# Softmax without the row-maximum pass in a two-block attention kernel, with a check of the row sums and a general program beside it

## The chip, the cores and the metric

The kernel runs on one core of one Trainium2 chip. The time is device microseconds (us) of one execution; medians of several executions are quoted, and one more execution of each kernel was recorded with a profile and a trace. All profiled executions and all timed ones named here were at a mean granted TensorE clock of 0.96 to 1.00. Engine names are those of the profile: PE is TensorE and PEld its weight loads, DVE is VectorE, ACT is ScalarE, POOL is GpSimd, SP is SyncE, SPq the queue of loads that SyncE issues.

## The reference

Two attention blocks over cached keys and values, A with grouped heads and B with one key and value head for each query head, their outputs set side by side:

```python
# A: Hq=32, Hkv=4 (each key/value head serves 8 query heads); B: 32 heads of each
# both: B=16, Sq=32, D=1024, Sk=1024, Dh=128, everything in bfloat16
q = (x @ wq).reshape(B, Sq, Hq, Dh).transpose(0, 2, 1, 3)
k = jnp.repeat(k_cache, rep, axis=1)          # rep = 8 in A, no repeat in B
v = jnp.repeat(v_cache, rep, axis=1)
scores = jnp.einsum("bhqd,bhkd->bhqk", q, k) * (Dh ** -0.5)
p = jax.nn.softmax(scores, axis=-1)
o = jnp.einsum("bhqk,bhkd->bhqd", p, v)
out = o.transpose(0, 2, 1, 3).reshape(B, Sq, Hq * Dh) @ wo
# ... and jnp.concatenate([a, b], axis=-1)
```

Inputs are normal numbers times 0.1, so the scores are small. B's keys and values are 268 MB of the 338 MB that have to be read.

## The kernel before

The work is cut into 128 "quads" of A and 128 of B. A quad is a block of 128 rows by 1024 scores: scores (TensorE), maximum (VectorE), exponential with row sum (ScalarE), transposes of P (TensorE), P times V (TensorE), normalisation, a transpose of the result, and now and then a projection. B's keys are transposed by VectorE, A's by TensorE. One load of 1 MB brings B's keys of a quad into one of two slots.

```python
NVB_SLOTS = 3
NKB_SLOTS = 2
DMA_BW = 330.7e3                      # bytes per us that the scheduler assumes
DUR = {                               # durations that the scheduler assumes, us
    "scoresB": 1.1, "scoresA": 0.45, "PT_trA": 0.50, ...
    "exp": 1.12, ...
    "KBt_tr": 1.15, "max": 1.17, "recip": 0.07, ...
}
# ... cut ...
def st_ktrB(q, t_):                   # frees the key slot rs
    sl, rs = q.kvslot, q.krslot
    pr.add("dve", lambda e: e.transpose(KBt_sb[:, sl, t_, :].bitcast(F32), KB_sb[:, rs, t_, :].bitcast(F32)),
           reads=[("KB", rs)], writes=[("KBt", sl, t_)], name="KBt_tr", ...)
# ... cut ...
def st_max(q):                        # minus scale times the row maximum, into stat
    sbf, sl = q.sbuf, q.slot
    pr.add("dve", lambda e: e.tensor_scalar(P_sb[:, sl, :], ps_s[:, sbf, :, :].rearrange("p u n -> p (u n)"), -scale, None,
                                            ALU.mult, ALU.min, accum_out=stat[:, sl, 0:1]),
           writes=BK_S[sbf] + [("nbias", sl), ("P", sl)], name="max", ...)

def st_exp(q):
    ...
    pr.add("act", lambda e: e.activation(dst, src, ACTF.Exp, bias=stat[:, sl, 0:1], scale=scale, accum_out=stat[:, sl, 1:2]),
           reads=[("nbias", sl)], writes=BK_S[sbf] + [("P", sl), ("rowsum", sl)], name="exp", ...)
```

Nothing of this is emitted as it is written. `pr.add` records operations with what they read and write. A list scheduler then goes through them with a small model: one in-order queue for each engine, the durations of `DUR`, one DMA pipe of `DMA_BW`. At each step it takes the ready operation with the earliest start (within 0.35 us, the one with the longest path behind it). The order it finds is emitted, with semaphore waits where the records ask for them.

```python
def list_schedule(self, lat=0.12, dma_bw=DMA_BW, dma_lat=1.8, look=0.35):
    # ... cut ...
    seq = sorted(range(n), key=lambda k: (ops[order[k]].t0, k))
    newp = Prog()
    for k in seq:
        eng, emit, reads, writes, dma_key, name, dur, tag, prio = self.specs[order[k]]
        newp.add(eng, emit, reads, writes, dma_key, name, dur, tag, prio)
    return newp
```

So an operation that is taken out of the program is also taken out of the scheduler's model, and every engine's order may come out differently.

## Time and profile before

| | before |
|---|---|
| median of the runs | 997.39 us at first, 995.62 with the later run (988.38 to 999.15) |
| span of the profiled run | 994.8 us |
| DMA queue of loads | 92.8% of 16 engines' span, 339.78 MB |
| VectorE, TensorE, ScalarE busy | 782.3, 863.6, 605.3 us |
| idle DMA, from stretches of 2 us | 11.3 us before 76 us, 59.4 in the middle, 19.3 in the last 75 |

The last line is read this way: cut the span into stretches of 2 us, take the DMA share of each, and add up what it lacks to 1. The prediction shows the other lines and how they hang together. These are the main rows of before's waits that belong to the softmax (columns: the waiter, whom it waited for, us in total, times, longest):

```profile
ACT P_sb L792 <- DVE P_sb L780: 99.6, 107, 5.6
...
PEld ps_pt L806 <- ACT P_sb L792: 26.4, 39, 3.1
...
DVE stat L843 <- ACT P_sb L792: 16.8, 26, 1.5
```

The first row is the exponential behind the maximum. The second is the transpose of P on TensorE, which needs the exponential's result; the third the reciprocal on VectorE, which needs its row sum.

### The profile page before, as it was taken

What the parts mean: (1) busy time and instruction counts of PE and PEld (TensorE: products, weight loads), DVE (VectorE), ACT (ScalarE), POOL (GpSimd) and SP (SyncE); (2) the same over time, 40 slices, a digit from 0 to 9 for tenths busy, and PEclk for the clock granted to TensorE, in tenths of its full rate; (3) what the DMA queues carried; (4) which work ended last, traced back from release to release, by engine and by line L of the source; (5) the groups of instructions that cost most, each with busy time, mean ns of one, the idle gap of its engine ahead of it and who ended that gap; (6) DMA issues with size and microseconds to landing.
All of it is one profiled execution on the core that took longest, in us unless ns stands there. A gap on an engine that the chain in (4) does not pass through costs nothing.

```text
span 994.8 us, 29548 instructions
## 1 busy us (share of the span) xinstructions
PE 863.6 (87%) x12864; PEld 480.5 (48%) x12864; DVE 782.3 (79%) x1460; ACT 605.3 (61%) x1237; POOL 1.1 (0%) x8
## 2 busy tenths in 40 slices
PE   5789999998998899998898989899988888888766
PEld 3345554555554555555454445455554445454332
DVE  2468787788887889888888788788887878988763
ACT  2247676766675667666575567657565656676332
POOL 0000000000000000000000000000000000000000
PEclk7999999999999999999999999999999999999875
DMA  8889899989999889999899997999999889999993
GB/s 306 306 300 375 327 352 349 386 329 357 355 350 393 331 323 389 357 366 366 315 382 384 344 354 268 347 378 349 357 368 386 306 316 363 377 352 354 337 339 141
DMA packets 151936, 341.66 MB, mean 343 GB/s; under 512 B 10496, under 2 KB 26880, under 8 KB 151808
## 3 DMA queue, kind: packets, MB, share of 16 engines
q1 hardware_dynamic: 151808, 339.78, 92.8%
q8 instruction: 101, 1.65, 0.7%
q14 instruction: 27, 0.22, 0.1%
HBM read 337.64 MB, written 2.10 MB: 342 GB/s over the span
## 4 chain that ended last, share of the span: by engine, by line
PE 47%; DVE 33%; ACT 14%; issue 2%; DMA 2%; SPq 0%; DVEq 0%; ACTq 0%
DVE P_sb L780 14%; DVE KBt_sb L733 12%; PE ps_s L769 9%; PE ps_pt L806 9%; ACT P_sb L792 8%; PE ps_pj L624 6%; PE ps_o L824 5%; PE ps_pj L546 4%; PE ps_pj L563 4%; ACT PT_sb L477 3%; PE ps_o L834 3%; PE ps_s L747 3%; DVE acc L637 2%; PE ps_o L860 2%; ACT KTA_sb L477 1%
## 5 line engine op out<-in xcount | busy, mean ns | idle before, releaser
L780 DVE TENSOR_SCALAR_CACHE_REDUCE P_sb<-ps_s 128x1024 bf16<-128x1024 f32 x256 | 310.0, 1213 | 80.5 <-PE ps_s L747 31.7
L792 ACT ACTIVATE P_sb<-ps_s,stat 128x1024 bf16<-128x1024 f32 x256 | 285.5, 1116 | 115.1 <-DVE P_sb L780 99.6
L733 DVE STREAM_TRANSPOSE KBt_sb<-KB_sb 128x1024 f32<-128x1024 f32 x256 | 309.8, 1226 | 5.9 <-PE ps_s L769 5.2
L477 ACT COPY PT_sb<-ps_pt 128x512 f32<-128x512 f32 x256 | 149.8, 585 | 92.6 <-PE ps_pt L806 74.2
L806 PE MATMUL ps_pt<-id,P_sb 128*128 128x128 f32 x1024 | 185.9, 305 | 19.7 <-ACT P_sb L792 13.7
L806 PEld LDWEIGHTS ps_pt<-id,P_sb 128*128 128x128 f32 x1024 | 149.8, 209 | 58.4 <-ACT P_sb L792 26.4
L769 PE MATMUL ps_s<-KBt_sb,QR 32*32 32x512 bf16 x4096 | 159.4, 402 | 18.0 <-DVE KBt_sb L733 12.8
L834 PE MATMUL ps_o<-VB_sb,PT_sb 128*32 128x128 bf16 x4096 | 85.8, 225 | 12.8 <-DVE OTA_sb L479 5.9
L747 PE MATMUL ps_s<-KTA_sb,QT_sb 128*128 128x512 bf16 x256 | 86.8, 385 | 5.1 <-ACT KTA_sb L477 1.6
L849 ACT ACTIVATE O_sb<-ps_o,stat 128x128 bf16<-128x128 f32 x128 | 47.2, 369 | 71.3 <-PE ps_o L824 64.4
L834 PEld LDWEIGHTS ps_o<-VB_sb,PT_sb 128*32 128x32 bf16 x4096 | 62.0, 99 | 56.8 <-issue 47.6
L769 PEld LDWEIGHTS ps_s<-KBt_sb,QR 32*32 32x32 bf16 x4096 | 49.6, 90 | 77.1 <-issue 25.5
L824 PE MATMUL ps_o<-VA_sb,PT_sb 128*128 128x128 bf16 x1024 | 79.7, 221 | 7.1 <-ACT OTB_sb L477 5.1
L824 PEld LDWEIGHTS ps_o<-VA_sb,PT_sb 128*128 128x128 bf16 x1024 | 62.9, 99 | 42.4 <-ACT OTB_sb L477 21.2
L624 PE MATMUL ps_pj<-woB_sb,OTB_sb 128*128 128x512 bf16 x256 | 76.7, 403 | 5.5 <-DVE ost L640 1.9
L563 PE MATMUL ps_pj<-wq_sb,xT_sb 128*128 128x512 bf16 x256 | 72.1, 392 | 5.5 <-ACT QR L477 3.5
L624 PE MATMUL ps_pj<-woA_sb,OTA_sb 128*128 128x512 bf16 x256 | 70.1, 382 | 6.4 <-DVE OTA_sb L479 5.7
L860 PE MATMUL ps_o<-ident,O_sb 128*128 128x128 bf16 x256 | 58.3, 228 | 18.0 <-DVE O_sb L853 15.4
L546 PE MATMUL ps_pj<-xT_sb,wq_sb 128*128 128x512 bf16 x256 | 68.8, 387 | 4.8 <-ACT QR L477 1.7
L860 PEld LDWEIGHTS ps_o<-ident,O_sb 128*128 128x128 bf16 x256 | 25.1, 98 | 81.5 <-DVE O_sb L853 38.6
L477 ACT CAST QR<-ps_pj 128x256 bf16<-128x256 f32 x128 | 48.0, 375 | 23.7 <-PE ps_pj L583 22.5
L853 DVE TENSOR_SCALAR O_sb<-ps_o,stat 128x128 bf16<-128x128 f32 x128 | 42.7, 334 | 17.8 <-PE ps_o L834 17.2
(37 smaller groups left out, 599.9 us busy)
## 6 DMA issues: line engine op xcount, KB each, us to landing
KB_sb<-in_B_k_cache_dram SPq DMA_DIRECT2D x128, 1024.0 KB, 7.3
VB_sb<-in_B_v_cache_dram SPq DMA_DIRECT2D x256, 512.0 KB, 8.5
KA_sb<-in_A_k_cache_dram SPq DMA_DIRECT2D x64, 256.0 KB, 9.0
VA_sb<-in_A_v_cache_dram SPq DMA_DIRECT2D x64, 256.0 KB, 8.5
wq_sb<-in_B_wq_dram SPq DMA_DIRECT2D x32, 256.0 KB, 8.2
wq_sb<-in_A_wq_dram SPq DMA_DIRECT2D x32, 256.0 KB, 7.5
woB_sb<-in_B_wo_dram SPq DMA_DIRECT2D x32, 256.0 KB, 9.6
woA_sb<-in_A_wo_dram SPq DMA_DIRECT2D x32, 256.0 KB, 8.6
```

Source lines behind the costliest of these rows:

```text
L477: pr.add("act", lambda e: e.copy(dst_ap, src_ap), reads=reads, writes=writes, name=name + "@act", wtag=wtag, rtag=rtag)
L546: last = e.matmul(ps_pj[:, 0:tn], wq_sb[:, 0, j, hc * Dh:(hc + 1) * Dh], xT_sb[:, 0, j, t0:t0 + tn], start=(j == 0), stop=(j == DJ - 1))
L563: last = e.matmul(ps_pj[:, 0:CW], xT_sb[:, 1, j, G * P:(G + 1) * P], wq_sb[:, 1, j, :], start=(j == 0), stop=(j == DJ - 1))
L624: last = e.matmul(ps_pj[:, 0:OUTW], OT[:, gp, hh, :], wo_[:, hh, oh * OUTW:(oh + 1) * OUTW], start=(hh == 0), stop=(hh == nh - 1))
L733: pr.add("dve", lambda e: e.transpose(KBt_sb[:, sl, t_, :].bitcast(F32), KB_sb[:, rs, t_, :].bitcast(F32)), reads=[("KB", rs)], writes=[(" ...
L747: pr.add("pe", lambda e, u=u: e.matmul(ps_s[:, sbf, u, :], qt[:, q.b, q.hh0:q.hh0 + 4, :].rearrange("p a q -> p (a q)"), KTA_sb[:, sl, u * ...
L769: last = e.matmul(ps_s[32 * cg:32 * cg + 32, sbf, g2, :].rearrange("p (s j) -> p s j", s=16), lhsT, rhs, start=(fp == 0), stop=(fp == 3), ...
L780: pr.add("dve", lambda e: e.tensor_scalar(P_sb[:, sl, :], ps_s[:, sbf, :, :].rearrange("p u n -> p (u n)"), -scale, None, ALU.mult, ALU.mi ...
L792: pr.add("act", lambda e: e.activation(dst, src, ACTF.Exp, bias=stat[:, sl, 0:1], scale=scale, accum_out=stat[:, sl, 1:2]), reads=[("nbias ...
L806: last = e.transpose(ps_pt32[:, m * P:(m + 1) * P], p32[:, m:Sk // 2:NPK], id32[:])
L824: last = e.matmul(OREG[0][0][:, 0:Dh], ptc, VA_sb[:, kvs, c, :], start=(c == 0), stop=(c == NCH - 1))
L834: last = e.matmul(ps_o[32 * a:32 * a + 32, 0:Dh], ptc, VB_sb[:, kvs, a // 2, a % 2, c, :], start=(c == 0), stop=(c == NCH - 1), tile_posit ...
```

## The change

The intent: softmax gives the same result with any constant subtracted in place of the maximum as long as nothing overflows or vanishes. The changed kernel subtracts nothing, so VectorE loses 256 passes over 128x1024 scores, and the exponential loses its wait for them. To stay right for any input, the reciprocals of all row sums are kept and compared with two limits at the end; if one lies outside, a slow general program with the maximum runs in the same launch.

```diff
+RINV_LOW, RINV_HIGH = 1e-10, 1e10
@@ ... cut ...
+    def whole(name, eng):
+        fast.run_engine(name, eng, fast_sems)
+        eng.wait_ge(fast_sems[flag_op.eng], flag_op.sig)
+        reg = eng.alloc_register("flag_" + name)
+        eng.reg_load(reg, flag[0:1, 0:1])
+        if name == "sp":
+            fast.await_dmas(eng, fast_sems)
+        with eng.If_ne(reg, flag_good):
+            eng.drain().then_inc(meet, 1)
+            eng.wait_ge(meet, len(engines))
+            general.run_engine(name, eng, general_sems)
@@ ... cut: the general program ...
-        def st_max(q):
-            sbf, sl = q.sbuf, q.slot
-            pr.add("dve", lambda e: e.tensor_scalar(P_sb[:, sl, :], ps_s[...], -scale, None, ALU.mult, ALU.min, accum_out=stat[:, sl, 0:1]), ...)
@@ st_exp
-            pr.add("act", lambda e: e.activation(dst, src, ACTF.Exp, bias=stat[:, sl, 0:1], scale=scale, accum_out=stat[:, sl, 1:2]),
-                   reads=[("nbias", sl)], writes=BK_S[sbf] + [("P", sl), ("rowsum", sl)], name="exp",
+            pr.add("act", lambda e: e.activation(dst, src, ACTF.Exp, scale=scale, accum_out=stat[:, sl, 1:2]),
+                   writes=BK_S[sbf] + [("P", sl), ("rowsum", sl)], name="exp",
@@ st_recip
-            pr.add("dve", lambda e: e.reciprocal(stat[:, sl, 2:3], stat[:, sl, 1:2]), ...)
+            pr.add("dve", lambda e: e.reciprocal(q.rinv, stat[:, sl, 1:2]), ...)      # a column of rinv_all
@@ before the scheduler
+        def st_check():
+            # ... cut: two comparisons of rinv_all with accum_out into good[:, 0:1] and good[:, 1:2], a memset of ones ...
+            pr.add("pe", lambda e: e.matmul(ps_pj[0:1, 0:2], ones[:], good[:], start=True, stop=True), ...)
+            # ... cut: two products on VectorE ...
+            pr.add("dve", lambda e: e.tensor_copy(flag[:], good[0:1, 1:2]), reads=[("good", 1)], writes=["flag"], name="flag")
+        st_check()
+        pr = pr.list_schedule()
```

`DUR` and `DMA_BW` stay as they were. The scheduler runs on a program in which the maximum does not exist.

## The prediction

> **What bounds the kernel now.** I read the page first, then the DMA queue's own waits, then stretches of 25 us and of 2 us, then the timeline where the DMA falls idle. From the page, engine totals, the load queue and the chain of waits:
>
> ```profile
> PE 863.6 (87%) x12864; PEld 480.5 (48%) x12864; DVE 782.3 (79%) x1460; ACT 605.3 (61%) x1237; POOL 1.1 (0%) x8
> ...
> q1 hardware_dynamic: 151808, 339.78, 92.8%
> ...
> PE 47%; DVE 33%; ACT 14%; issue 2%; DMA 2%; SPq 0%; DVEq 0%; ACTq 0%
> DVE P_sb L780 14%; DVE KBt_sb L733 12%; PE ps_s L769 9%; PE ps_pt L806 9%; ACT P_sb L792 8%; PE ps_pj L624 6%; PE ps_o L824 5%; PE ps_pj L546 4%; PE ps_pj L563 4%; ACT PT_sb L477 3%; PE ps_o L834 3%; PE ps_s L747 3%; DVE acc L637 2%; PE ps_o L860 2%; ACT KTA_sb L477 1%
> ...
> L780 DVE TENSOR_SCALAR_CACHE_REDUCE P_sb<-ps_s 128x1024 bf16<-128x1024 f32 x256 | 310.0, 1213 | 80.5 <-PE ps_s L747 31.7
> L792 ACT ACTIVATE P_sb<-ps_s,stat 128x1024 bf16<-128x1024 f32 x256 | 285.5, 1116 | 115.1 <-DVE P_sb L780 99.6
> L733 DVE STREAM_TRANSPOSE KBt_sb<-KB_sb 128x1024 f32<-128x1024 f32 x256 | 309.8, 1226 | 5.9 <-PE ps_s L769 5.2
> ```
>
> No engine fills the span, but the DMA engines nearly do: 92.8% for loads alone. The chain blames TensorE and VectorE in turns; its 14% on the maximum (L780) is 139 us, which is an upper bound and not the gain, since a DMA at 92.8% stands beside it. The maximum and the transpose of B's keys (L733) are two equal blocks on one in-order VectorE.
>
> The link between VectorE and the DMA is in the DMA queue's own waits (columns: waiter and releaser, us in total, times, longest):
>
> ```profile
> SPq L700 <- DVE KBt_sb L733: 262.3, 67, 13.6
> SPq L700 <- DVE stat L843: 112.7, 22, 10.1
> SPq L700 <- DVE O_sb L853: 54.1, 14, 7.7
> ```
>
> L700 loads a megabyte of B's keys into one of two slots; a slot is free once VectorE has transposed it. The names behind the arrow are whichever VectorE instruction brought its counter to the awaited value. That wait is harmless while the queue still has transfers to work off. Two stretches of 25 us show when it is not (the last columns are granted clock, DMA share, GB/s):
>
> ```profile
> 300.00:325.00 25.00, 21.47 (x314) 12.34 (x314) 19.17 (x36) 14.70 (x32) 0.00 (x0) 1.00 1.04 392
> 600.00:625.00 25.00, 22.89 (x354) 12.78 (x353) 21.23 (x39) 16.14 (x33) 0.00 (x0) 1.00 0.75 271
> ```
>
> At 300 the DMA runs full at 392 GB/s; at 600 it is empty for a quarter of the time, and TensorE is no less busy. I cut the first 960 us into stretches of 2 us: in 358 of 480 the share was at least 0.98, at a mean of about 387 GB/s; the shortfall of the others from a share of 1 adds up to 75 us: 11 before 76 us, 59 between 76 and 920, 5 after. I looked at what the queue waited for in 14 places where the share fell: in 13 it was an L700 load released by VectorE. One of them, around 570 us:
>
> ```profile
> 567.90 1.23 DVE L780 TENSOR_SCALAR_CACHE_REDUCE P_sb<-ps_s 128x1024 bf16<-128x1024 f32 x1 [0.71 <-PE ps_s L769]
> ...
> 569.78 2.36 DVE L733 STREAM_TRANSPOSE KBt_sb<-KB_sb 128x1024 f32<-128x1024 f32 x2
> ...
> 572.17 0.37 SPq L700 DMA_DIRECT2D KB_sb<-in_B_k_cache_dram  x1
> ```
>
> The DMA share is 0.09 at 570 to 572. The two transposes stand behind the maximum and its wait for scores; the load goes out the moment they end.
>
> **What the Trainium skill says.** "VectorE: DVE Perf Modes", section on the TRN2 errata, gives 120 + elements cycles at 0.96 GHz for a source in PSUM: 1192 ns for 1024 elements at one per cycle. The trace has 1213, so the maximum is already at the rate of its form and only its removal helps. "ScalarE: Activation LUTs", section "What ACT_TABLE_LOAD costs", puts about 93 ns on each per-partition pointer operand of an activation. The trace agrees: the 128x128 normalisation with a pointer scale takes 369 ns, the 128x128 copy 269. "DMA: Bandwidth & Descriptors", Specifications, names about 358 GB/s as a core's HBM limit; this trace holds 392 over 25 us with one core running, so I use the measurement. "Runtime: NRT & Kernel Launch", "Instruction fetch mechanics", says a taken branch outside the prefetched window must fetch its target before execution goes on, without a figure; no such branch is in this trace.
>
> **The change part by part.**
>
> 1. Removed: 256 maxima of 1213 ns and 256 accumulator reads of 83 ns on VectorE: 310 + 21 = 331 us. VectorE falls to 782 - 331 = 451 us, under half of any likely span.
>
> 2. Removed from each softmax: 1.2 us plus 0.1 between the scores and the exponential, and VectorE's queueing on top. ScalarE's idle time before exponentials caused by the maximum, 99.6 us, should vanish; part of it returns as a wait for scores.
>
> 3. The built program gives the exponential an immediate bias in place of a pointer. At about 95 ns each, 256 of them take 24 us off ScalarE: 1116 to about 1020 ns, ScalarE 605 to about 581 us. It was idle 39% of the time, so this alone is worth little.
>
> 4. Added: results of the reciprocal go to columns of one tile (same size, no cost); two checks of 128x256, one 1x2 matmul, three tiny VectorE operations, and one register load, compare and taken branch on every engine. In the instruction order, the matmul and the last three VectorE operations stand behind the last accumulation, beside the last store, which took some 2.7 us in the trace (992.1 to 994.8). I estimate 1 to 4 us for what sticks out, 2.5 in the middle. The general program is skipped; its instructions cost only the jump.
>
> 5. Moved: the scheduler rebuilds the order. The counts on TensorE and the DMA queue stay the same apart from the check, and A's work stays in the same ratio to B's (17 quads of A by B's 16th, 122 by its 112th), so I expect no new shape.
>
> What then sets the end? TensorE: from start-to-start distances around 500 to 510 us, B's 32 score matmuls take 1.07 us, B's values 0.57, four transposes of P about 0.6, A's scores 0.43, A's values 0.45, a transpose of A's keys 0.45 per two quads, the shuffle 0.22, the output transposes 0.06 each, and eight projection matmuls 1.72: about 6.0 us per pair, times 128 is 770 us of dense work. The DMA needs 341.66 MB / 387 GB/s = 883 us. So the DMA is the next bound, TensorE comes 13% behind it.
>
> The sum: 883, plus 2 before the first byte, plus some 19 after the last load has landed (about 976 to 994.8), is 904 us, a floor. The span of 994.8 lies 91 above it: 75 of idle DMA, and 16 of reduced rate. Idle DMA in the middle, 59, should shrink to about 20, since VectorE's other in-order waits for TensorE and ScalarE stay in front of the transposes (saves 39). The start, paced by TensorE's projections and small loads, gives back 2; reduced rate 5; the B-only end 1.5; the last two softmaxes in the drain 2.4. Together 50, less 2.5 for the check: 47.5. From the median of 997.4: about 950 us.
>
> **The rivals.**
>
> The DMA is hidden-bound already and VectorE's load is worth nothing. For it: 92.8%, and the megabytes stay. Against it: 13 of 14 gaps end with VectorE, and full stretches run 14% faster than the mean of 343 GB/s. It would leave 985 to 995 us.
>
> The wait moves to TensorE: key slots still free late, because transposes stand behind reciprocals, normalisations and accumulations that wait for matmuls, and value slots (L713, L707) wait for TensorE as now (39.7 and 25.0 us). For it: TensorE is 87% busy and its share is rarely under 80%. Against: 770 us of dense work. It would keep most of the 59 and give 965 to 980.
>
> The full gain: two in-order engines stop blocking one another and the DMA saturates through the middle: 905 to 925 us. For it: stretches such as 300 to 325 do that with VectorE at 77%.
>
> A dear exit, with tens of us for branch and fetch, would be seen only at the end; I give it little.
>
> **Range and chances.** Between the full gain and TensorE's in-order waits I take 950, and 925 to 975 eight times in ten; the three times before themselves differ by 1%. Two per cent faster means under 977.4: only the first rival, or the second at its worst, fails that. Faster 0.91, same 0.08, slower 0.01.
>
> **What would show it.** Right: DMA share of loads 96 to 98% and a mean near 360 GB/s; VectorE near 450 us; exponential near 1020 ns; the L700 wait on VectorE well under 262 us; the chain of waits with no maximum and more TensorE, and DMA above its 2%. Wrong: a rate in full stretches under 380 GB/s (contention), the share still 93% with gaps released by TensorE (second rival), or an exit of over 5 us after the last store.

## The result, and the profile after

The changed kernel's median is 958.87 us (955.75 to 961.89, 4 runs), before's in the same session 995.62. Ratios here are the mean time of one kernel's fast runs over that of the other's of the same rounds, so they are not quite the ratio of the medians; for the change it is 0.964 (95% interval 0.9588 to 0.9692). The result is correct, and the general program did not run.

The page of the changed kernel, engine totals, the load queue, the chain of waits and two groups:

```profile
PE 850.0 (89%) x12866; PEld 473.5 (49%) x12866; DVE 503.5 (53%) x955; ACT 576.0 (60%) x1237; POOL 1.3 (0%) x10
...
q1 hardware_dynamic: 151808, 339.78, 94.9%
...
PE 65%; ACT 24%; DVE 6%; issue 2%; DMA 2%; SPq 0%; POOLq 0%; DVEq 0%
...
L846 DVE STREAM_TRANSPOSE KBt_sb<-KB_sb 128x1024 f32<-128x1024 f32 x256 | 308.3, 1225 | 38.3 <-PE ps_s L882 27.2
L899 ACT ACTIVATE P_sb<-ps_s 128x1024 bf16<-128x1024 f32 x256 | 263.8, 1030 | 83.3 <-PE ps_s L882 53.7
```

VectorE is free for half of the span, and its share of the chain fell from 33% to 6%. The exponential (L899) takes 1030 ns in place of 1116. But the loads fill only 94.9%, and the chain went to TensorE and ScalarE, not to the DMA, whose 2% did not move. The question for the trace is who empties the DMA now. Two stretches of 25 us, the same as in the prediction (the last columns are granted clock, DMA share, GB/s):

```profile
300.00:325.00 25.00, 23.19 (x329) 12.71 (x327) 12.97 (x26) 14.37 (x31) 0.00 (x0) 1.00 1.05 410
600.00:625.00 25.00, 22.53 (x347) 12.93 (x344) 13.44 (x27) 17.32 (x37) 0.00 (x0) 1.00 0.93 342
```

The same parts of the work do not lie at quite the same times, so this shows only the kind: a full stretch runs at 410 GB/s, and others are still not full. By stretches of 2 us the idle DMA of the middle fell from 59.4 to 42.8 us, that of the last 75 us from 19.3 to 12.9, that of the start stayed (11.3 and 11.6). The load queue's own waits in the changed kernel:

```profile
SPq L813 <- DVE KBt_sb L846: 189.4, 54, 13.7
SPq L813 <- DVE rinv_all L950: 188.6, 41, 8.9
SPq L813 <- DVE OTA_sb L590: 56.2, 16, 7.6
SPq L826 <- PE ps_o L941: 49.3, 30, 5.6
```

L813 is the load of B's keys. The names behind the arrow can't be taken at their word. In the built program every such load that waits for VectorE waits for the count of a key transpose; and in the trace 121 of the 126 loads that reuse a slot start within 0.1 us of the end of that slot's second transpose (116 before). A reciprocal, 0.15 us long, has nothing to do with keys: it is named because it runs beside the transpose. So the rows have to be added up: over all VectorE instructions, L813 waited 465 us, and L700 before 500.

A plainer measure, from the trace, is how long a slot is held: from the landing of a key load to the end of its second transpose. That is 7.18 us on average, before 7.35. In all the time in which some slot is held so, VectorE idles 345 us, before 144. The removed work left VectorE, waits came in its place, and the slots come free hardly sooner. VectorE is still late, and now not because it is busy. Its own waits say why:

```profile
DVE OTA_sb L590 <- PE ps_o L967: 92.9, 86, 3.9
DVE O_sb L960 <- PE ps_o L941: 89.7, 89, 3.7
DVE rinv_all L950 <- ACT P_sb L899: 87.5, 89, 4.4
...
PEld ps_pt L913 <- ACT P_sb L899: 48.4, 76, 1.7
```

The reciprocal (L950) waits 87.5 us for exponentials, where it waited 16.8 before. The first two rows, waits for TensorE, were 21.3 and 17.2. TensorE's transposes of P wait 48.4 us for them, before 26.4. Whatever stands behind such a wait in the same queue waits as well, B's key transposes among it. I looked at 12 of the places where the DMA share falls; in 11 a key load released by VectorE ends the gap. One of them, from the timeline (start, us, engine and operation; in brackets the idle time before it and who ended it):

```profile
671.20 0.69 DVE L748 TENSOR_TENSOR acc<-acc,ps_pj 128x512 f32<-128x512 f32 x1 [1.37 <-PE ps_pj L735]
...
674.79 0.69 DVE L748 TENSOR_TENSOR acc<-acc,ps_pj 128x512 f32<-128x512 f32 x1 [1.75 <-PE ps_pj L735]
...
675.60 1.22 DVE L846 STREAM_TRANSPOSE KBt_sb<-KB_sb 128x1024 f32<-128x1024 f32 x1
...
676.85 0.37 SPq L813 DMA_DIRECT2D KB_sb<-in_B_k_cache_dram  x1
```

The DMA share is 0.24 at 674 to 676. VectorE stands still for 1.75 us, waiting for a projection, and the key transpose stands behind the accumulation in its order. The load goes out when that transpose ends, though the table of waits puts this load's 8.9 us down to a reciprocal. The wait shown is for a projection, not for an exponential; in-order waits of both kinds add up.

The end of the program, before first:

```profile
991.39 0.69 DVE L640 TENSOR_TENSOR ost<-acc,ps_pj 128x512 bf16<-128x512 f32 x1 [1.99 <-PE ps_pj L624]
992.11 0.33 SPq L643 DMA_DIRECT2D out_dram<-ost  x1
```

And of the changed kernel:

```profile
950.86 0.69 DVE L751 TENSOR_TENSOR ost<-acc,ps_pj 128x512 bf16<-128x512 f32 x1 [1.98 <-PE ps_pj L735]
951.57 0.33 SPq L754 DMA_DIRECT2D out_dram<-ost  x1
...
951.69 0.19 PE L1136 MATMUL ps_pj<-good,ones 128*1 128x2 f32 x2 [0.87 <-DVE ost L751]
...
952.28 0.14 DVE L1142 CAST flag<-good 1x1 int32<-1x1 f32 x1
```

From the end of the last accumulation to the end of the span it is 994.8 - 992.08 = 2.7 us before and 957.3 - 951.55 = 5.75 after. The flag is done at 952.4. The store takes 2.0 us from issue to landing in both, so it lands at 953.6, and 3.7 us follow it, where 0.7 followed it before. In SyncE's program only the compare and the branch stand behind that landing; they leave no row. No engine works in those 3.7 us (953.6 to 957.3), and instruction packets are all that the DMA moves (queue: packets, MB, share):

```profile
q14 instruction: 5, 0.04, 3.6%
q8 instruction: 1, 0.02, 1.6%
```

So the check itself hides beside the store, and the exit costs 3.0 us; how it divides between the engines' register loads, compares and branches isn't resolved.

### The profile page after: what moved, and what is told of

Same layout as the page of the kernel before. It is cut to its first block, busy times and chain, and to the rows that moved or that the text cites. A ratio compares the mean times of both kernels' runs of the same rounds, so it can differ in the third digit from the quotient of the medians.

```text
span 957.3 us, 29084 instructions
## 1 busy us (share of the span) xinstructions
PE 850.0 (89%) x12866; PEld 473.5 (49%) x12866; DVE 503.5 (53%) x955; ACT 576.0 (60%) x1237; POOL 1.3 (0%) x10
## 3 DMA queue, kind: packets, MB, share of 16 engines
q1 hardware_dynamic: 151808, 339.78, 94.9%
## 4 chain that ended last, share of the span: by engine, by line
PE 65%; ACT 24%; DVE 6%; issue 2%; DMA 2%; SPq 0%; POOLq 0%; DVEq 0%
PE ps_pt L913 14%; ACT P_sb L899 13%; PE ps_s L882 12%; PE ps_pj L735 9%; PE ps_o L941 7%; PE ps_pj L657 6%; ACT PT_sb L588 5%; PE ps_pj L674 5%; PE ps_o L931 5%; PE ps_s L860 3%; DVE KBt_sb L846 3%; PE ps_kt L837 2%; ACT QR L588 2%; ACT KTA_sb L588 1%; PE ps_o L967 1%
## 5 line engine op out<-in xcount | busy, mean ns | idle before, releaser
L899 ACT ACTIVATE P_sb<-ps_s 128x1024 bf16<-128x1024 f32 x256 | 263.8, 1030 | 83.3 <-PE ps_s L882 53.7
L913 PEld LDWEIGHTS ps_pt<-id,P_sb 128*128 128x128 f32 x1024 | 147.4, 208 | 76.6 <-ACT P_sb L899 48.4
L882 PE MATMUL ps_s<-KBt_sb,QR 32*32 32x512 bf16 x4096 | 171.0, 400 | 10.5 <-ACT QR L588 8.5
L960 DVE TENSOR_SCALAR O_sb<-ps_o,rinv_all 128x128 bf16<-128x128 f32 x128 | 44.1, 345 | 90.4 <-PE ps_o L941 89.7
L941 PEld LDWEIGHTS ps_o<-VB_sb,PT_sb 128*32 128x32 bf16 x4096 | 59.8, 97 | 60.9 <-issue 44.9
L950 DVE RECIPROCAL rinv_all<-stat 128x1 f32<-128x1 f32 x256 | 37.9, 150 | 95.8 <-ACT P_sb L899 87.5
L882 PEld LDWEIGHTS ps_s<-KBt_sb,QR 32*32 32x32 bf16 x4096 | 47.4, 89 | 76.9 <-issue 41.1
L735 PE MATMUL ps_pj<-woB_sb,OTB_sb 128*128 128x512 bf16 x256 | 73.1, 386 | 5.4 <-DVE ost L751 2.6
L590 DVE COPY OTA_sb<-ps_o 128x128 bf16<-128x128 bf16 x128 | 27.9, 218 | 93.4 <-PE ps_o L967 92.9
L748 DVE TENSOR_TENSOR acc<-acc,ps_pj 128x512 f32<-128x512 f32 x64 | 43.8, 684 | 48.9 <-PE ps_pj L735 48.8
```

Of the source, the lines that this page charges most:

```text
L735: last = e.matmul(ps_pj[:, 0:OUTW], OT[:, gp, hh, :], wo_[:, hh, oh * OUTW:(oh + 1) * OUTW], start=(hh == 0), stop=(hh == nh - 1))
L882: last = e.matmul(ps_s[32 * cg:32 * cg + 32, sbf, g2, :].rearrange("p (s j) -> p s j", s=16), lhsT, rhs, start=(fp == 0), stop=(fp == 3), ...
L899: pr.add("act", lambda e: e.activation(dst, src, ACTF.Exp, scale=scale, accum_out=stat[:, sl, 1:2]), writes=BK_S[sbf] + [("P", sl), ("rows ...
L913: last = e.transpose(ps_pt32[:, m * P:(m + 1) * P], p32[:, m:Sk // 2:NPK], id32[:])
L941: last = e.matmul(ps_o[32 * a:32 * a + 32, 0:Dh], ptc, VB_sb[:, kvs, a // 2, a % 2, c, :], start=(c == 0), stop=(c == NCH - 1), tile_posit ...
```

## The experiments

The open question after the first look: did the change earn little because VectorE's work was worth little, or did something give part of the gain back? Three theories. The first (load): VectorE's work was in the way, and what is gained is what the removed work cost. The second (link): the exponential's wait for VectorE was in the way, and the work would have been harmless. The third (order): both were worth more than 37 us, and the new order of instructions, found by a scheduler that no longer knows of any delay between scores and exponential, gives part of it back. The third came out of x4's result.

To talk about orders I use one number, taken from the built programs and not from a profile: for each quad, the TensorE work that stands in program order between its scores and the transposes of its P, each instruction counted at the distances that the prediction lists. The mean over 256 quads is 3.74 us before and 2.04 us after. In the changed kernel TensorE comes back for P after 2 us, and an exponential takes 1.03 us plus its queue.

Twelve kernels ran, all correct. Times are medians of 4 runs; the ratio is to before, in the same rounds. "Loads" is the share of the load queue.

| run | what it is | us | ratio (95%) | loads |
|---|---|---|---|---|
| after | the change | 958.87 | 0.964 (0.9588 to 0.9692) | 94.9% |
| x1_dve_load | after, dead VectorE load in place of the maximum | 976.81 | 0.9815 (0.9776 to 0.9853) | 93.5% |
| x2_link_only | after, exponential waits for a tiny maximum | 957.56 | 0.9609 (0.9573 to 0.9646) | 94.6% |
| x4_old_order | after, in the order of before | 928.08 | 0.9319 (0.9287 to 0.9352) | 96.4% |
| x7_exp_slack | after, scheduler thinks exponentials long | 962.71 | 0.9659 (0.9622 to 0.9696) | 95.1% |
| x8_dve_room | after, scheduler leaves room on VectorE | 950.93 | 0.9553 (0.9521 to 0.9586) | 95.3% |
| x10_old_load | x4 with the dead load | 969.76 | 0.9748 (0.9714 to 0.9783) | 93.6% |
| x11_old_link | x4 with the tiny maximum | 938.6 | 0.9427 (0.9395 to 0.9458) | 95.6% |
| x12_latency_only | after, scheduler knows a delay before the exponential | 939.47 | 0.945 (0.9421 to 0.9479) | 95.3% |
| h_sp | after, loads in the order of before | 963.84 | 0.9696 (0.9658 to 0.9735) | 93.7% |
| h_pad | x4, loads in the order of after | 952.97 | 0.9574 (0.952 to 0.9629) | 94.2% |
| x13_old_bw | x4, scheduler's DMA rate 395 GB/s | 914.58 | 0.9203 (0.9166 to 0.9239) | 98.2% |
| x14_before_bw | before, scheduler's DMA rate 395 GB/s | 962.56 | 0.9691 (0.9652 to 0.9729) | 96.2% |

Before's median drifted from 996.16 to 993.0, so I compare by ratios; 0.01 is 10 us.

### x1_dve_load: the work back, without the wait

A VectorE instruction of the maximum's form and size, from one SBUF tile to another. It waits for the scores, as the maximum did, and nobody reads its result; only the next scores in the same buffer have to wait for it, which in the trace they did 3 times, for 2.3 us in all. A form that read the scores themselves beside the exponential could not be used: a race, since two engines would read one PSUM bank with nothing to order them.

```diff
+        def st_max(q):
+            sbf, sl = q.sbuf, q.slot
+            pr.add("dve", lambda e: e.tensor_scalar(junk[:], xT_sb[:, 0, 0:2, :].rearrange("p j t -> p (j t)"), -scale, None,
+                                                    ALU.mult, ALU.min, accum_out=stat[:, sl, 0:1]),
+                   reads=[("Sd", sbf), ...], writes=["junk", ("nbias", sl)], name="max", rtag={("Sv", sbf): q.qid})
@@ both steps, behind st_scores(q)
+            st_max(q)
```

> The changed kernel with a dead VectorE instruction of the maximum's length (1.2 us, 256 of them, SBUF to SBUF, nobody reads the result) put back behind each score block. The exponential does not wait for it. Theory 1, VectorE's queue: the work in front of the key transposes is what cost the time, so most of the gain is lost: 982 to 995 us, ratio to the kernel before 0.985 to 1.00, and the loads' DMA share back at 93%. Theory 2, the softmax's latency: the shorter way from scores to exponential is what paid, so the gain stays: 956 to 966 us, ratio 0.96 to 0.97. A split in between would say that both carry.

Measured: 976.81 us, ratio 0.9815, so 18 us of the 37 are lost again, between the two zones written down for it (the verdict at 2% is "unclear", since the interval holds 0.98). The dead load's own row on the page:

```profile
L894 DVE TENSOR_SCALAR_CACHE_REDUCE junk<-xT_sb 128x1024 bf16<-128x1024 bf16 x256 | 309.8, 1210 | 50.2 <-PE ps_s L883 39.5
```

It has the maximum's length (1210 ns against 1213), so it is a fair stand-in for its time on the engine. It fills a gap that VectorE would otherwise idle through in part, and it still costs half of the gain. VectorE's work is in the way. The order of the program is new here as well, and it is, instruction for instruction, the order of x8 below, which runs without the load in 950.93 us. So in that order the load costs 26 us, of which the order itself had won back 8.

### x2_link_only: the wait back, without the work

```diff
+        def st_max(q):
+            pr.add("dve", lambda e: e.tensor_scalar(P_sb[:, sl, 0:8], ps_s[:, sbf, 0, 0:8], -scale, None,
+                                                    ALU.mult, ALU.min, accum_out=stat[:, sl, 0:1]), ..., name="max8", ...)
@@ st_exp
-            ... ACTF.Exp, scale=scale, accum_out=stat[:, sl, 1:2]),
+            ... ACTF.Exp, bias=stat[:, sl, 0:1], scale=scale, accum_out=stat[:, sl, 1:2]),
+                   reads=[("nbias", sl)], ...
```

> The changed kernel with the maximum taken over 8 of the 1024 columns (a valid shift of the exponent, so the result stays right): the exponential waits for VectorE as before and takes a pointer bias, but VectorE does only some 0.25 us for it. Theory 1, VectorE's queue: the gain stays but for the 60 us or so of added small VectorE work: 960 to 972 us, ratio 0.965 to 0.977. Theory 2, latency: the wait for a place in VectorE's queue comes back, and with it most of the loss: 980 to 992 us, ratio 0.983 to 0.997.

Measured: 957.56 us, 0.9609: nothing lost, and below both zones. The minimum over 8 columns takes 160 ns, and the exponential with its pointer bias 1117 ns again. In this order, which was made with the short maximum in the model (0.2 us), a wait of the exponential for VectorE is free, and so are 27 us more of ScalarE (603.2 against 576.0). It doesn't follow that the link was free before: this order is another one. The mean distance from scores to transposes is 2.6 us here, half a microsecond more than after, because the scheduler knew of the step.

### x4_old_order: the change in the order of before

The maximum is in the program while the scheduler runs and is dropped afterwards. Each engine's order was compared: it is that of before, without the maximum.

```diff
@@ list_schedule, at the end
-            newp.add(eng, emit, reads, writes, dma_key, name, dur, tag, prio)
+            if name != "max":
+                newp.add(eng, emit, reads, writes, dma_key, name, dur, tag, prio)
@@
+        def st_max(q):
+            pr.add("dve", None, writes=BK_S[sbf] + [("nbias", sl), ("P", sl)], name="max")
@@ st_exp: reads=[("nbias", sl)]; both steps: st_max(q) behind st_scores(q)
```

> The changed kernel, scheduled with the maximum in place and the maximum then dropped: the order of all other instructions is that of the kernel before. If the gain is the removed work and wait, 955 to 968 us, ratio 0.958 to 0.972. If the gain comes from the scheduler's new order, 975 us or more, ratio 0.98 or above.

Measured: 928.08 us, 0.9319, far below both zones: I had asked whether a new order made the gain, and it took some of it away. This is the run that decides. The same instructions as in the changed kernel, in another order, take 31 us less. The change itself is worth 68 us (996 to 928), and its new order gives 31 back. Its page:

```profile
PE 835.6 (90%) x12866; PEld 475.4 (51%) x12866; DVE 499.7 (54%) x955; ACT 577.5 (62%) x1237; POOL 1.3 (0%) x10
...
q1 hardware_dynamic: 151808, 339.78, 96.4%
...
PE 65%; ACT 15%; DMA 8%; DVE 8%; issue 2%; SPq 1%; POOLq 0%; DVEq 0%; ACTq 0%
```

The counts are those of the changed kernel to the instruction (12866, 955, 1237). The DMA has entered the chain with 8%. Four of its waits, to be set against 87.5, 48.4, 189.4 and 188.6 of the changed kernel:

```profile
DVE rinv_all L955 <- ACT P_sb L904: 28.1, 39, 4.4
...
PEld ps_pt L918 <- ACT P_sb L904: 17.9, 31, 1.7
```

```profile
SPq L814 <- DVE KBt_sb L847: 266.5, 74, 14.7
SPq L814 <- DVE rinv_all L955: 86.4, 23, 9.7
```

TensorE and VectorE wait much less for exponentials. (VectorE's copies of the result, OTA_sb, wait more for TensorE, 153.5 us against 92.9.) The key loads' waits for VectorE, all names together, fall from 465 to 413 us, and a key slot is held 5.80 us in place of 7.18. The idle DMA of the middle is 29.7 us, against 42.8.

### x10_old_load and x11_old_link: the two parts in the order of before

Now the same two questions as in the first two runs, with the order held. x10 puts the dead load where the maximum stood, x11 the tiny maximum with the exponential waiting.

```diff
@@ x10: list_schedule, at the end: the dead load keeps only its wait for the scores
+            if name == "max":
+                sbf = writes[0][1] // 2
+                reads, writes = [("Sd", sbf)], ["junk"]
@@ x11: st_max over 8 columns as in x2, scheduled with the full maximum's duration
```

> The order of the kernel before on all engines, with a dead VectorE instruction of the maximum's length in each maximum's place (source and result in SBUF), for which the exponential does not wait. With the order held fixed this gives back VectorE's load without the softmax's wait. Theory 1, load in front of the key transposes: most of the 68 us between the kernel before and the old order without the maximum come back, 975 to 995 us, ratio 0.98 to 1.0. Theory 2, latency: 928 to 940 us, ratio 0.93 to 0.945. From the first batch, where the dead load cost 18 us in the new order, I expect some 945 to 960.

> The order of the kernel before on all engines, with each maximum taken over 8 columns: the exponential still waits for VectorE and has its pointer bias, VectorE's load is 0.25 us in place of 1.3. Theory 1, load: near the old order without the maximum, 930 to 945 us, ratio 0.935 to 0.95. Theory 2, latency and the wait for a place in the queue: 965 to 990 us, ratio 0.97 to 0.995.

Measured: 969.76 us (0.9748) with the load alone, 938.6 us (0.9427) with the link alone, against 0.9319 with none and 1 with the real maximum. In order: the load costs 43 us (between its two zones), the link 11 (in the zone of theory 1), both together 68, so some 14 belong to neither alone. From x10's page:

```profile
q1 hardware_dynamic: 151808, 339.78, 93.6%
...
L897 DVE TENSOR_SCALAR_CACHE_REDUCE junk<-xT_sb 128x1024 bf16<-128x1024 bf16 x256 | 308.5, 1205 | 65.5 <-PE ps_s L886 32.3
```

All that the trace shows waiting for these 256 instructions is one normalisation, for 1.2 us; and yet the loads fall from 96.4% to 93.6%, and a key slot is held 7.08 us in place of 5.80: work that delays the key transposes delays the key loads. (The comparison with before is not quite clean: x4, x10 and x11 have the check, 3 us, which before has not, and x4 and x10 have the immediate bias, which x11 and before have not. Before's full stretches of DMA are also slower than those of x4 and x10, as the last section shows, and the 14 us may be that and no interplay; no run parts them.) The first theory is right for most of the gain, and the second for a sixth.

### x7_exp_slack: a wrong way to give the scheduler its delay back

If the order is bad because the scheduler sees no delay, a longer exponential in its model should mend it. Only the model's duration changes.

```diff
-    "exp": 1.12, "PT_ev@act": 0.52, ...
+    "exp": 2.41, "PT_ev@act": 0.52, ...
```

> The changed kernel with one number altered: the scheduler is told that the exponential lasts 2.41 us instead of 1.12. No instruction is added or taken; TensorE's order now has 4.6 us of its own work on average between a score block and the transposes of its P, against 2.0 in the changed kernel and 3.7 in the kernel before. Theory 3, the new order starves TensorE: its in-order queue reaches the transposes of P before the exponential is done, so this recovers most of the 30 us between the changed kernel and the old order: 925 to 940 us, ratio 0.93 to 0.945. Rival, VectorE's new order (no gaps left where the maximum stood) is at fault: 950 to 960 us, ratio 0.955 to 0.965.

Measured: 962.71 us, 0.9659: a miss for both zones, no better than the changed kernel. The distance rose to 4.6 us, more than before's, and it did not help. The load queue's waits show what it cost:

```profile
SPq L826 <- PE ps_o L941: 104.0, 53, 5.4
...
SPq L820 <- PE ps_o L931: 78.1, 50, 7.5
```

These are loads of values, whose slots TensorE frees after P times V; L826 waited 49.3 us for it in the changed kernel. The edit did not only add a delay, it also made ScalarE full in the model: 256 exponentials of 2.41 us are 617 us where 287 were. The scheduler then pushed everything behind ScalarE later. So the run doesn't refute the order; it shows that more distance is not better by itself, and that a delay must not be modelled as work.

### x8_dve_room and x12_latency_only: room on VectorE, or a delay

x8 is scheduled with the dead load of x1, which takes VectorE's time but whose result nobody reads; it is dropped afterwards. x12 is scheduled with a step of 1.17 us between scores and exponential on an engine that doesn't exist, so that it takes nobody's time; it too is dropped.

```diff
@@ both: dropped at the end of list_schedule, as in x4
+            if name != "max":
@@ x12
+            pr.add("nobody", None, writes=BK_S[sbf] + [("nbias", sl), ("P", sl)], name="max")
```

> The changed kernel scheduled with a dead maximum on VectorE that nobody waits for, and the dead work dropped afterwards: VectorE's order is made with room for it, but TensorE's distance between scores and transposes of P stays short (2.1 us of work on average). Theory 3, distance on TensorE: no better than the changed kernel, 950 to 965 us, ratio 0.955 to 0.968. Rival, VectorE's order: 925 to 940 us, ratio 0.93 to 0.945.

> A cleaner form of the run that lengthened the exponential, which in the scheduler's model also filled ScalarE: here the scheduler sees a step of 1.17 us between scores and exponential on an engine that does not exist, dropped afterwards, so TensorE has 3.7 us of work between scores and the transposes of P (the kernel before has the same 3.7), but VectorE's order is made without room for a maximum. Theory 3, distance on TensorE is what the new order lost: 925 to 938 us, ratio 0.93 to 0.942. Rival, room in VectorE's order is needed too: 945 to 960 us, ratio 0.95 to 0.965.

Measured: 950.93 us (0.9553) with room, 939.47 us (0.945) with the delay, against 0.964 in the new order and 0.9319 in the old. Room on VectorE gives 9 of the 32, the delay 19; together 28, near the whole; with intervals of 3 to 5 us on each, that they add up isn't shown. The delay alone fell between the two zones: it is the larger part, not the whole. The distances agree with the edits, 2.07 us in x8 and 3.71 in x12. One row of each table of waits, x8 first:

```profile
DVE rinv_all L958 <- ACT P_sb L907: 120.6, 98, 4.4
```

```profile
DVE rinv_all L955 <- ACT P_sb L904: 42.1, 48, 4.4
```

With room but no delay, VectorE waits for exponentials even longer than in the changed kernel (120.6 against 87.5); with the delay half as long. What that does to the key slots, from the traces (mean time held; VectorE's idle time while some slot is held):

| run | slot held, us | VectorE idle meanwhile, us |
|---|---|---|
| before | 7.35 | 144 |
| after | 7.18 | 345 |
| x7, longer exponential in the model | 7.17 | 347 |
| x8, room | 7.04 | 343 |
| x12, delay | 5.82 | 237 |
| x4, order of before | 5.80 | 238 |
| x13, x4 with a faster DMA in the model | 5.63 | 218 |
| x10, x4 with the dead load | 7.08 | 121 |

The delay alone brings the slots free as early as the old order does. Room alone does not; by what path it gains its 9 us stays open.

### h_sp and h_pad: is it the order of the loads, or that of the engines?

Orders of TensorE, VectorE and ScalarE could not be mixed: taken from two schedules they contradict one another and the program can't be built. The load queue's order can be parted from them.

```diff
@@ instead of pr.list_schedule(): the old order for some engines, the new one for the others
+OLD_ORDER_ENGINES = ('sp',)                     # h_sp
+OLD_ORDER_ENGINES = ('pe', 'act', 'dve')        # h_pad
+        pr = merge_orders(pr, OLD_ORDER_ENGINES)
```

> The changed kernel's order on TensorE, ScalarE and VectorE, with the DMA queue's order of the kernel before. If the order of the loads is what the new schedule spoiled, 925 to 940 us, ratio 0.93 to 0.945; if it is the compute engines' order, 950 to 965 us, ratio 0.955 to 0.968.

> The reverse: the order of the kernel before, without the maximum, on TensorE, ScalarE and VectorE, with the changed kernel's order of the loads. If the compute engines' order carries the 30 us, 925 to 940 us, ratio 0.93 to 0.945; if the order of the loads does, 950 to 965 us, ratio 0.955 to 0.968.

Measured: 963.84 us (0.9696) with the old loads under the new order, a little worse than the changed kernel, though the intervals overlap; 952.97 us (0.9574) with the new loads under the old order, 25 us worse than x4. Neither order is the cause alone: put back by itself, the old order of the loads gives nothing, and the old order of the engines gives 7 of the 32. From h_pad's load queue:

```profile
SPq L872 <- PE ps_o L991: 76.7, 35, 6.0
```

This is a load of values again, 37.9 us in x4 for the same wait. A load that waits for its slot holds up those behind it in the queue; that this is where the 25 us went is argued, not shown. The two orders are parts of one schedule and fit each other.

### x13_old_bw and x14_before_bw: the model's DMA rate

In full stretches (DMA share at least 0.98) the trace of before moves 388 GB/s, while the scheduler assumes 330.7. x13 is x4 with the measured figure of the changed kernels; x14 is before with nothing else changed.

```diff
-DMA_BW = 330.7e3
+DMA_BW = 395e3
```

> A try for a better version: scheduled with the maximum in place and the maximum dropped, as in the fastest run so far, with the scheduler's DMA rate raised from 330.7 to 395 GB/s, which is nearer what the full stretches show. If the model's slow DMA holds TensorE's order back, 915 to 925 us, ratio 0.918 to 0.928; if the order is already good enough, 925 to 935 us, ratio 0.928 to 0.94.

> The kernel before, maximum and all, with the scheduler's DMA rate raised from 330.7 to 395 GB/s, one number. Beside the run with the maximum dropped from the same order (914.6 us) it tells what the removal is worth in this order. If VectorE's queue in front of the key transposes is the limit, the better load order helps little while the maximum is there: 980 to 995 us, ratio 0.985 to 1.0, and the removal is worth 65 to 80 us. If the order of the loads was the limit by itself: 960 to 978 us, ratio 0.967 to 0.983.

Measured: x13 914.58 us, 0.9203, the best version of all and faster than both kernels, just below its zone. Its page:

```profile
span 912.8 us, 29140 instructions
...
q1 hardware_dynamic: 151808, 339.78, 98.2%
...
PE 64%; DMA 12%; ACT 12%; DVE 8%; issue 2%; SPq 1%; POOLq 0%; ACTq 0%; DVEq 0%
```

Idle DMA in the middle is 17.7 us. The floor that the prediction estimated is 904.

x14: 962.56 us, 0.9691, where my main expectation was 980 to 995. One number in the scheduler, with the maximum in place, is worth nearly what the change was worth. Its VectorE is as busy as before's:

```profile
PE 854.5 (89%) x12864; PEld 478.0 (50%) x12864; DVE 779.5 (81%) x1460; ACT 603.8 (63%) x1237; POOL 1.1 (0%) x8
...
q1 hardware_dynamic: 151808, 339.78, 96.2%
```

So a VectorE at 81% and loads at 96.2% go together, if the order suits. That is a limit on the first theory: how much the maximum's work costs depends on the order around it. With the better rate in the model, removing the maximum with the order kept is worth 962.6 - 914.6 = 48 us, with the old rate 68.

## Why the prediction was right or wrong

The predicted time, 950 us, is 9 us from the measured 958.9, inside the range. The account of it was wrong in one step and off in several sizes, and two of the errors cancel, so that it came so near is in part luck.

**The bound.** Right. The loads stayed the nearest to full, and a key load waiting for VectorE ends nearly every gap, as before. Two readings were off: the names behind the arrow of the L700 waits, which are not the instructions that the loads wait for (see the profile after), and the last landing, which the traces put near 979.5 and not 976, so that the floor of 904 is some 3 us high. The best version shows where that leads: loads at 98.2%, the DMA in the chain with 12%.

**Part 1, VectorE.** The sign was right, the size off: 503.5 us, not 451. The busy time on the page is a union of intervals, in which consecutive instructions overlap; the durations of the groups are a sum. Before, the groups add up to 864 us and the page says 782.3. The groups' sum fell by 329 us, as predicted (331), and the union by 279. A sum was subtracted from a union. It did no harm, since VectorE was not the bound.

**Parts 2 and 3, the exponential.** Its wait of 99.6 us for the maximum is gone, and part of it came back as 53.7 for scores. Its length fell from 1116 to 1030 ns, 86 ns where about 95 were predicted (the two groups that the prediction compared, 369 and 269 ns, also differ in the type of their source; this pair does not); ScalarE's total is 576.0 us where 581 was. I have no run of the immediate bias alone, so what it is worth in time stays open; x2 lost nothing by giving it up.

**Part 4, the exit.** Right in size: 3.0 us, in the range of 1 to 4. But not where it was expected: the check's matmul and VectorE operations hide beside the store, and what sticks out comes after its landing. It was read from the two traces; a run without the check was not made.

**Part 5, the order.** This is the step that failed: "so I expect no new shape". The counts were indeed the same, and A's place beside B's too (17 quads by B's 16th, 122 by its 112th, in the built programs), but the order was not. x4 measures it: the new order costs 31 us. The mechanism, as far as the runs show it: with the maximum gone from the model, the scheduler puts the transposes of P 2.0 us of TensorE work behind their scores, not 3.7. TensorE and VectorE then wait longer in order for exponentials (VectorE 87.5 us against 28.1 in x4), and VectorE for P times V (89.7 against 63.9): with a key slot held, VectorE idles 345 us in place of 238 in the old order, and a slot is held 7.18 us in place of 5.80, so the loads go out later. x12 (a delay in the model, nothing else) recovers 19 us of it, and the whole of the slot time; x8 (room on VectorE) 9. Why just these two distances suit the rest of the program is not settled, and x7 shows that more distance is not simply better.

**The sum.** Its terms, set against the traces (idle DMA from stretches of 2 us; the rate from 341.7 MB at 388 and at 395 GB/s, 880.6 and 865.0 us):

| term | predicted | after | x4, order kept |
|---|---|---|---|
| idle DMA in the middle | 39 | 59.4 - 42.8 = 17 | 59.4 - 29.7 = 30 |
| start | 2 | 0 | 0 |
| rate | 5 | 16 | 28 (at 401 GB/s) |
| tail and drain | 3.9 | 19.3 - 12.9 = 6 | 19.3 - 14.1 = 5 |
| check and exit | -2.5 | -3.0 | the same code, -3.0 taken over |
| sum | 47.5 | 36 | 60 |
| span, measured | | 994.8 - 957.3 = 37.5 | 994.8 - 926.2 = 68.6 |

For the changed kernel the account closes to 2 us; for x4 it misses 8. The middle was forecast at 20 us of idle DMA and kept 42.8; even in the kept order it keeps 29.7. The rate was forecast as a small term and is as large as the middle. That the rate rose is measured, that the removal of the maximum raised it is not shown. So the removal was underrated (47.5 forecast, 68 measured) and the reordering was forecast as free and costs 31; 68 - 31 = 37.

**The rivals.** "DMA hidden-bound" fell: the gain is there. "The wait moves to TensorE" had the right kind, since VectorE now waits in order for TensorE and ScalarE and a key slot is held 7.18 us where it was 7.35; and in the new order its figure of 965 to 980 was near. But value slots are not the main waiter (49.3 us of L826 beside 465 of L813), and it isn't a property of the change, as x4 shows. "The full gain", 905 to 925, needs the order kept and the model's rate corrected: x13, 914.6.

**The tests that I named.** Loads at 96 to 98%: missed, 94.9%. A mean near 360 GB/s: 357. VectorE near 450: missed. Exponential near 1020 ns: nearly, 1030. The key loads' wait on VectorE well under 262: in its letter yes (189.4 under the transposes' name), in its sense no, since all names together fell only from 500 to 465. No maximum in the chain and more TensorE: met, 65% for 47%. DMA in the chain above 2%: missed, and met in x4 and x13. Of the signs of being wrong, full stretches under 380 GB/s and gaps released by TensorE did not come. An exit of over 5 us after the last store did in its letter, counted from the end of the store's issue (957.3 - 951.9 = 5.4 us; 3.7 from its landing), though what it adds to before is 3.0. The share of loads, the slot waits and the DMA in the chain point at the order; the 450 us was a fault of the sum.

## What to carry to other kernels

Where a scheduler builds the order, taking an operation out is two changes: schedule once with it and drop it afterwards, and compare, before judging what its removal is worth. A gain that is smaller than the removed work, with in-order engines waiting for one another where the work was, was the sign of it here; and the constants of the scheduler's model, here a DMA rate 15% under the measured one, can be worth as much as the change.

## What the Trainium skill lacked or had wrong

- "DMA: Bandwidth & Descriptors", section "Where 436 GB/s comes from", says that for transfers from HBM to SBUF the HBM side of about 358 GB/s binds. With one core running, the runs show otherwise: 388 to 401 GB/s in full stretches, and a mean of 374 GB/s over the whole span of x13. "Perfetto Trace Analysis", section "Roofline", has it as these runs do: one active core can draw more than its 358, up to a ceiling of its DMA engines, some 120% in practice; 401 is 112%.
- No page says why full stretches differ in rate. At equal DMA share (1.04 to 1.06), before and x14 move 393 GB/s, and the changed kernel, x4, x10 and x13 move 404 to 407 (x7, without a maximum too, 400). The first two have the real maximum, and x10, with as busy a VectorE on SBUF data, doesn't share their rate; so it isn't VectorE's time as such. But the first two are also the only ones without the check and the general program, and no run parts the two. What it is stays open, and by the sum above it is worth some 16 us of the 37.
- "Runtime: NRT & Kernel Launch", section "Instruction fetch mechanics", warns that a taken branch has to fetch its target, without a figure (another page times a compare and a branch, but not the fetch). The skipped general program, the register load and the check together cost 3.0 us at the end here (5.75 us after the last accumulation in place of 2.7). All of it lies behind the landing of the last store, where six instruction packets are the only traffic, which agrees with the page; the branch's own part is not resolved.
- No page that I read deals with what a change does to a list-scheduled order: the same instructions took 958.9 us in one order and 928.1 in another.
